# Cosine-weighted linear attention with a token-mixing layer: one load DMA of 576 KB in place of two of 288 KB

## The chip, the cores and the metric

The kernel runs on one core of a Trainium2 chip. The metric is the time of one execution on the device, in microseconds (us). A core has a matrix engine (TensorE, PE), a vector engine (VectorE, DVE), a scalar engine (ScalarE, ACT), a general engine (GpSimd, POOL) and an engine that here only issues transfers (SyncE, SP). Each runs its own instructions in order. The transfers themselves are carried by 16 DMA engines.

## The reference

Inputs are q, k and v of shape (batch 8, heads 8, positions 576, width 64) in float32, and three weights. The first stage is linear attention with cosine and sine weights on the positions, the second mixes tokens by products of two projections:

```python
theta = pi/2 * arange(576)/576
phi(x) = concat([relu(x)*cos(theta), relu(x)*sin(theta)], -1)
kv  = einsum('bhsf,bhsd->bhfd', phi(k), v);  z = sum(phi(k), axis=2)
x   = (phi(q) @ kv) / (phi(q) @ z + 1e-6)          # heads side by side: (8, 576, 512)
W   = (x @ w_q) @ (x @ w_k).T / sqrt(64)
out = relu(W @ x) @ w_out                          # (8, 576, 512) float32
```

## The kernel before

**Tiling.** The work is cut into 16 half batches, H = 0 to 15. A half batch is four heads of one batch, two pairs of heads. For each of q, k and v it has a raw tile of 128 partitions x 2 pairs x 576 float32 values (2304 B per partition and pair, 294912 B = 288 KB per pair). A pair of heads lies in DRAM as one contiguous block, 2304 B per partition; the two pairs of a half batch are two such blocks, one behind the other. Four raw tiles per tensor are used in turn (`NRAW` = 4), so the load of half batch H overwrites the tile of H - 4 and has to wait until that one was read.

**Stages of a half batch.** `L` loads (line 132). `RK`, `RQ` (relu to bf16, lines 187 and 189) and `CV` (cast, lines 193 and 195) read the raw tiles on ACT or POOL. `VS` (line 213, DVE) multiplies v by the table of cosines and sines; `QT` transposes q on PE, `QM` (line 253, DVE) weights it; `KV` (line 234, PE) forms the products of k and v, `KE` copies them out. `N` (line 269, PE) is the numerator with the denominator beside it, `EP` and `X` (lines 277 to 287) divide. Then, by batch: `XT` or `XR` transposes x and `XE` copies it, `WK`, `WQ`, `KX`, `MX` are matmuls of the second stage with copies `KW`, `QW`, `XK`, `XA`, `XB`, `ME` between them, `WO` (line 403, PE) is the product with the output weight, `OE` copies a 128 x 512 result into one of 12 output buffers, and `ST` (line 413) stores it (256 KB, 36 in all). `LW` loads the three weights (128, 128 and 1024 KB), `CW` casts them.

**Order.** The whole program is one list of words, `ORDER`, written out by hand or by a planner ahead of time and run through once. A word is a step, its index, the PSUM place (`:n`) and the engine (`@A`, `@V`, `@G`). Every engine takes its steps in the order of the list, and no step overtakes another on its engine. SP therefore has one order of loads and stores: a load whose tile is not yet free, or a store whose data isn't ready, holds all loads and stores behind it. Loads and stores together are 135 DMAs, all issued by SP.

**Halves.** Words with `a` or `b` (`LK0a`, `RK0b`) handle one pair of heads alone; they are used for half batch 0 only. Without it, `part` is `None`: a load then issues two DMAs, one per pair, and `RK`, `RQ`, `CV` and `VS` handle both pairs in one instruction. The list's first loads in SP's order are

```
LV1 LQ0b LQ1 LK1 LV0a LV0b LK0a LQ0a LK0b LV3 LQ3 LK3 LV2 LK2 LQ2 LV5 LW0 LW1 LK5 LQ4 LQ5 LV7 LV4
LQ7 LK4 LQ6 LW2 LV6 LK7 LV8 LK6 LV10 LQ8 LV9 LK10 LQ9 LK8 LK9 LQ11 LV11 LQ10 ST6 LK11 LV12 LK14 LK13
LV13 LQ12 LK12 LQ13 ST10 LV14 LV15 ST13 ST4 LQ14 ST3 LQ15 ST11 ST15 ST17 LK15 ST5 ...
```

and from there on only stores follow.

Of the kernel before, what the change touches and what calls it, by code (L numbers as in the profile page):

```python
# [63 lines left out]
def kernel(  # L64
# [10 lines left out]
    nc = tc.nc  # L75
# [18 lines left out]
    NRAW, NPREP, NV2, NQM, NX, NXT, NOUT = (4, 2, 2, 2, 2, 2, 12)  # L94
# [6 lines left out]
    def bufs(n, shape, dtype, name):  # L101
        return [pool.tile(shape, dtype, name=f"{name}{i}") for i in range(n)]

    raw = {nm: bufs(NRAW, [P, 2, HC], FP32, f"{nm}raw") for nm in "kqv"}
# [18 lines left out]
    def srcs(src):  # L123
        return [src[b].flatten().rearrange("(pr p e) -> p pr e", pr=NPAIR, p=P)
                for b in range(B)]

    src = {"k": srcs(k), "q": srcs(q), "v": srcs(v)}

    def load(nm, H, part):
        b, h = divmod(H, 2)  # L130
        for r in (0, 1) if part is None else (part,):
            nc.sync.dma_start(raw[nm][H % NRAW][:, r, :], src[nm][b][:, 2 * h + r, :])  # L132

# [300 lines left out]
    for word in ORDER.split():  # L434
        word, _, eng = word.partition("@")
        word, _, ps = word.partition(":")
        part = {"a": 0, "b": 1}.get(word[-1])
        word = word.rstrip("ab")
        kind = word[:2] if word[:2] in steps or word[0] in "LRCVT" else word[0]
        i, ps = int(word[len(kind):] or 0), int(ps or 0)  # L440
        if kind in ("LK", "LQ", "LV"):
            load(kind[1].lower(), i, part)
        elif kind in halves:
            halves[kind](i, ps, ENG.get(eng), slice(0, 2) if part is None else
                         slice(part, part + 1))
        else:
            steps[kind](i, ps, ENG.get(eng))
# [30 lines left out]
```

## Time and profile before

| | |
|---|---|
| time, median of 3 runs | 123.74 us (123.45 to 124.1) |
| the profiled execution | 122.49 us, of it a span of 120.7 us |
| granted TensorE clock | 0.991 of full speed |
| busy in the span | PE 94.8 us (79%), DVE 88.2 (73%), ACT 84.2 (70%), POOL 52.2 (43%) |
| moved | 39.40 MB, mean 326 GB/s |
| loads of q, k, v | 96 DMAs of 288 KB, median 5.9 to 6.0 us from issue to landing |
| stores | 36 DMAs of 256 KB, median 3.1 us |

The profile is one execution seen by the hardware's profiler. The span is the time from its first to its last instruction; the execution's own time is 1.8 us longer. In lines with instructions the first number is the start in us from the span's beginning, the second the duration, followed by the engine, the line of the kernel, the operation, and what it writes and reads; what stands in square brackets is idle time of the engine just before it and what ended it. A line of waits gives the total in us, how often, and the longest. SPq is SP's queue of DMA issues: a duration there is that of the issue, not of the transfer.

### The profile page before, as it was taken

The numbers are of one execution on the slowest core, as the hardware profiler recorded it, in microseconds if no ns is written. First come the engines' busy times: TensorE is split into PE (matmuls) and PEld (weight loads), VectorE is DVE, ScalarE is ACT, GpSimd is POOL, SyncE is SP. The second block draws the span as 40 slices with busy tenths as digits, with TensorE's granted clock in tenths as the row PEclk, the third lists the DMA queues.
The fourth block names the chain that finished last, engine by engine and source line by source line (L and its number), as shares of the span: only waits on it lengthen the run. The fifth ranks groups of instructions, "written<-read, shape, count | busy, mean of one in ns | idle before, by whom it ended". The sixth has DMA issues, their size and how long they took to land.

```text
span 120.7 us, 5301 instructions
## 1 busy us (share of the span) xinstructions
PE 94.8 (79%) x2286; PEld 63.1 (52%) x2286; DVE 88.2 (73%) x132; ACT 84.2 (70%) x155; POOL 52.2 (43%) x63
## 2 busy tenths in 40 slices
PE   0005919758778899969999999798999999999950
PEld 0004818637656656635667576454755864653410
DVE  0136998889989998997979987759969868766200
ACT  7246452967887989777967897586678668757450
POOL 2577136032739758146799304937365310010000
PEclk9999999999999999999999999999999999999996
DMA  3999999999999999999989999999997681875685
GB/s 111 318 384 405 395 391 391 361 405 396 392 390 408 398 337 344 355 360 379 383 282 326 364 285 391 343 331 283 391 299 263 238 329 55 320 288 198 237 331 196
DMA packets 20615, 39.40 MB, mean 326 GB/s; under 512 B 3184, under 2 KB 3184, under 8 KB 20592
## 3 DMA queue, kind: packets, MB, share of 16 engines
q1 hardware_dynamic: 20592, 39.07, 89.8%
q8 instruction: 18, 0.29, 1.0%
q14 instruction: 5, 0.04, 0.1%
HBM read 29.62 MB, written 9.44 MB: 324 GB/s over the span
## 4 chain that ended last, share of the span: by engine, by line
DMA 39%; PE 39%; DVE 6%; issue 4%; SPq 3%; ACT 3%; POOL 2%; DVEq 0%; ACTq 0%; POOLq 0%
DMA kraw<-in_k_dram 24%; PE ps L403 20%; DMA vraw<-in_v_dram 11%; DMA out_dram<-o 5%; PE ps L234 3%; PE ps L383 3%; PE ps L269 3%; SPq L132 3%; PE ps L360 3%; DVE v L213 2%; PE ps L313 2%; DVE x L287 2%; PE ps L245 2%; PE ps L333 2%; PE ps L346 2%
## 5 line engine op out<-in xcount | busy, mean ns | idle before, releaser
L403 PE MATMUL ps<-wow,mix 128*128 128x512 bf16 x144 | 34.7, 380 | 0.0
L287 DVE TENSOR_TENSOR x<-ps,rec 128x640 bf16<-128x640 f32 x32 | 26.4, 824 | 2.2
L195 POOL TENSOR_SCALAR vb<-vraw 128x1152 bf16<-128x1152 f32 (+1 forms) x16 | 17.9, 1122 | 20.9 <-DMA vraw<-in_v_dram 18.6
L213 DVE TENSOR_TENSOR v<-vb,vtab 128x2304 bf16<-128x2304 bf16 (+1 forms) x17 | 21.7, 1289 | 6.6 <-POOL vb L195 6.6
L253 DVE TENSOR_TENSOR qm<-ps,qtab 128x2304 bf16<-128x2304 bf16 x16 | 21.4, 1350 | 4.6 <-ACT qtab L166 2.9
L193 ACT COPY o<-ps 128x512 f32<-128x512 f32 x30 | 17.5, 587 | 6.6 <-PE ps L403 4.5
L269 PE MATMUL ps<-kvs,qm 64*128 64x65 bf16 x640 | 15.3, 199 | 6.0 <-ACT kvs L193 3.3
L403 PEld LDWEIGHTS <-mix 128*128 128x128 bf16 x144 | 12.4, 98 | 14.2 <-issue 0.9
L394 ACT ACTIVATE mix<-ps 128x576 bf16<-128x576 f32 x26 | 16.4, 657 | 3.2 <-PE ps L383 3.2
L189 POOL TENSOR_SCALAR rq<-qraw 128x1152 bf16<-128x1152 f32 x9 | 13.4, 1487 | 11.4 <-DMA qraw<-in_q_dram 10.8
L269 PEld LDWEIGHTS <-qm 64*128 64x128 bf16 x640 | 13.3, 100 | 9.4 <-issue 5.7
L189 POOL TENSOR_SCALAR rk<-kraw 128x1152 bf16<-128x1152 f32 (+1 forms) x12 | 13.8, 1150 | 9.4 <-DMA kraw<-in_k_dram 7.0
L193 ACT COPY xT<-ps 128x1280 bf16<-128x1280 bf16 (+1 forms) x13 | 15.4, 1186 | 3.3 <-PE ps L313 1.7
L234 PE MATMUL ps<-v,rk 64*64 64x130 bf16 x576 | 12.5, 236 | 3.0 <-DVE x L287 1.3
L245 PE MATMUL ps<-ident,rq 64*128 64x64 bf16 x288 | 7.6, 199 | 9.3 <-ACT rq L187 8.8
L187 ACT ACTIVATE rq<-qraw 128x1152 bf16<-128x1152 f32 (+1 forms) x8 | 8.4, 1046 | 6.6 <-DMA qraw<-in_q_dram 6.6
L234 PEld LDWEIGHTS <-rk 64*64 64x64 bf16 x576 | 10.1, 117 | 5.2 <-ACT rk L187 1.4
L245 PEld LDWEIGHTS <-rq 64*128 64x128 bf16 x288 | 6.1, 101 | 11.7 <-ACT rq L187 9.0
L383 PE MATMUL ps<-wq,kx 64*128 64x288 bf16 x64 | 8.3, 287 | 0.3 <-ACT xT L193 0.2
L195 POOL TENSOR_SCALAR kx<-kx 64x256 bf16<-64x256 bf16 x7 | 2.8, 399 | 12.6 <-ACT kx L193 12.2
L286 DVE RECIPROCAL rec<-rec 128x10 f32<-128x10 f32 x32 | 6.8, 211 | 1.8 <-ACT rec L277 1.4
L277 ACT ACTIVATE rec<-ps,eps 128x10 f32<-128x10 f32 x23 | 6.2, 273 | 1.7 <-PE ps L269 1.6
(46 smaller groups left out, 99.3 us busy)
## 6 DMA issues: line engine op xcount, KB each, us to landing
vraw<-in_v_dram SPq DMA_DIRECT2D x32, 288.0 KB, 6.0
qraw<-in_q_dram SPq DMA_DIRECT2D x32, 288.0 KB, 5.9
kraw<-in_k_dram SPq DMA_DIRECT2D x32, 288.0 KB, 5.9
out_dram<-o SPq DMA_DIRECT2D x36, 256.0 KB, 3.1
wof<-in_moe_w_out_dram SPq DMA_DIRECT2D x1, 1024.0 KB, 7.6
wqf<-in_moe_w_q_dram SPq DMA_DIRECT2D x1, 128.0 KB, 5.5
wkf<-in_moe_w_k_dram SPq DMA_DIRECT2D x1, 128.0 KB, 5.2
```

The costliest lines, as they stand in the source:

```text
L189: eng.tensor_scalar(dst, s, FMAX, 0.0, op0=ALU.min, op1=ALU.max)
L193: A.copy(dst, s)
L195: G.tensor_scalar(dst, s, 1.0, 1.0, op0=ALU.mult, op1=ALU.mult)
L213: V.tensor_mul(v2_b[H % NV2][:, part, :, :, 0:D], vb_b[H % NPREP][:, part].unsqueeze(3).to_broadcast([P, n, C, 2, D]), vtab.unsqueeze(1).t ...
L234: nc.tensor.matmul(kv_v[o, r, :], rk_b[H % NPREP][a, pr, c, :], v2_b[H % NV2][a, pr, c, :, 0:D + 1], start=(c == 0), stop=(c == C - 1))
L245: nc.tensor.transpose(qt_v[:, r, c * H2:(c + 1) * H2], rq_b[H % NPREP][a, c, :, :], ident[a, a])
L253: V.tensor_mul(qm_b[H % NQM][:, :, :, 0:C, :].rearrange("p s r c d -> p s r (c d)"), qt_view(place["QT", H]).unsqueeze(1).to_broadcast([P, ...
L269: nc.tensor.matmul(nv[:, pr, u, :], qm_b[H % NQM][a, s, r, 2 * u:2 * u + 2, :], kv_b[H % 2][a, r, s, 0:D + 1], start=(u == 0 and s == 0), ...
L287: V.tensor_tensor(x_b[b % NX][:, :, 4 * h:4 * h + 4, :].rearrange("p u (w r) d -> p r w u d", r=2)[:, r], nv[:, :, :, 0:D], rec.to_broadca ...
L383: nc.tensor.matmul(pair(ps)[:, t, :].bitcast(FP32)[:, 0:HS], kx_b[b % 2][a, (m // 2) ^ t, (m % 2) * P:(m % 2 + 1) * P], wq_b[b % 2][a, :], ...
L394: A.activation(dst, s, AF.Relu, scale=scale_moe)
L403: nc.tensor.matmul(o, mix_b[bp % 2][:, m, rt * P:(rt + 1) * P], wow[:, m, :], start=(m == 0), stop=(m == NDM - 1))
```

## The change

From half batch 2 on a load without a part is one DMA for both pairs of heads. Its destination is the whole raw tile, its source the two blocks of 2304 B per partition. Loads of half batches 0 and 1, the weights and the stores stay as they are, and so does the list. 42 loads are touched: 84 DMAs of 288 KB become 42 of 576 KB.

```diff
     def load(nm, H, part):
         b, h = divmod(H, 2)
+        if part is None and H > 1:
+            nc.sync.dma_start(raw[nm][H % NRAW], src[nm][b][:, 2 * h:2 * h + 2, :])
+            return
         for r in (0, 1) if part is None else (part,):
             nc.sync.dma_start(raw[nm][H % NRAW][:, r, :], src[nm][b][:, 2 * h + r, :])
```

## The prediction

> **What bounds the kernel now.** I read the page's slices first, to see which resource is full when; then the chain that ended last, to see which of them sets the end; then the waits of the DMA queue's issuer (SP), its issues in order of time, and the places where ACT, DVE and PE stand idle for a load.
>
> The page: busy tenths of PE and of the DMA engines in 40 slices of 3.02 us, what they moved, the shares of the chain, and the load issues.
>
> ```profile
> PE   0005919758778899969999999798999999999950
> DMA  3999999999999999999989999999997681875685
> GB/s 111 318 384 405 395 391 391 361 405 396 392 390 408 398 337 344 355 360 379 383 282 326 364 285 391 343 331 283 391 299 263 238 329 55 320 288 198 237 331 196
> DMA 39%; PE 39%; DVE 6%; issue 4%; SPq 3%; ACT 3%; POOL 2%; DVEq 0%; ACTq 0%; POOLq 0%
> kraw<-in_k_dram SPq DMA_DIRECT2D x32, 288.0 KB, 5.9
> ```
>
> Two regimes. Up to about 40 us the transfers run near 395 GB/s and PE is half idle; from about 50 us PE is full and transfers run at 280 to 390. The chain is loads until 32.8 us, compute until 61.6, loads again (64.4 to 76.4), one store (81.0 to 86.9), then PE.
>
> SP's waits (total us, times, longest), its issues in narrow windows, and steps of the chain (start, us):
>
> ```profile
> SPq L132 <- DMA qraw<-in_q_dram: 7.2, 19, 0.4
> SPq L132 <- DMA wof<-in_moe_w_out_dram: 2.2, 1, 2.2
> ...
> 10.75 0.33 SPq L132 DMA_DIRECT2D kraw<-in_k_dram  x1
> 16.01 0.33 SPq L132 DMA_DIRECT2D qraw<-in_q_dram  x1
> 37.19 0.33 SPq L132 DMA_DIRECT2D kraw<-in_k_dram  x1
> 39.71 0.33 SPq L132 DMA_DIRECT2D kraw<-in_k_dram  x1
> ...
> 26.28 6.51 DMA vraw<-in_v_dram
> 69.22 7.16 DMA kraw<-in_k_dram
> 81.00 5.93 DMA out_dram<-o
> ```
>
> SP waits for landings of loads that its next issue doesn't need as data. Counting the order out, the issue at 39.71 (second half of K6) is the eighth DMA after the 1 MB output weight, whose landing it waited for: a DMA is held until the one eight before it has landed. So eight are in flight, and 8 x 0.75 us is the 5.9 us to landing. The two K issues at 10.75 and the Q issue at 16.01 are seven places apart: (16.01 - 10.75) / 7 = 0.751 us for one 288 KB DMA, 393 GB/s. The issues at 37.19 and 39.71 follow two neighbouring landings, the second that of the 1 MB weight: 2.52 us, 416 GB/s.
>
> Where engines are idle for a load (DVE and ACT in order of time):
>
> ```profile
> 16.10 1.16 ACT L187 ACTIVATE rq<-qraw 128x1152 bf16<-128x1152 f32 x1 [2.41 <-DMA qraw<-in_q_dram]
> 21.13 1.16 ACT L187 ACTIVATE rk<-kraw 128x1152 bf16<-128x1152 f32 x1 [0.63 <-DMA kraw<-in_k_dram]
> 34.12 1.36 DVE L213 TENSOR_TENSOR v<-vb,vtab 128x2304 bf16<-128x2304 bf16 x1 [0.36 <-POOL vb L195]
> 76.49 1.16 ACT L187 ACTIVATE rk<-kraw 128x1152 bf16<-128x1152 f32 x1 [1.16 <-DMA kraw<-in_k_dram]
> 87.01 0.59 ACT L193 COPY o<-ps 128x512 f32<-128x512 f32 x1 [0.78 <-DMA out_dram<-o]
> ```
>
> These are RQ3, RK2, VS4 (through CV4 on POOL), RK12 and a copy into an output buffer whose store had not landed. They are short: loads are late by little.
>
> **The change part by part.** 84 DMAs of 288 KB become 42 of 576 KB. Bytes, order and readers stay. From the third half batch RK, RQ and CV each read both halves in one instruction, so no reader could use a first half before the second.
>
> *Transfer time.* Rate without overhead: (1048576 - 294912) B / (2.52 - 0.751) us = 426 GB/s; so a 288 KB DMA is 0.692 us of bytes and 0.059 us of its own. One 576 KB DMA then takes 1.443 us where two take 1.502: 0.059 us saved per load. Bounds: nothing saved, if the weight's rate comes from something else than its size; and below nothing, since eight DMAs before the landing at 76.38 (69.22 to 76.38) took 0.895 us each with the queue full: at that rate a load is 0.29 us slower. I take 0.059, because the weight is also one DMA of several separated rows per partition (four rows of 2048 B; here two of 2304 B), the nearest row. [...]
>
> *What that does to 34 us.* Two merged loads (V3, Q3) lie before RQ3: it starts 0.12 us earlier, and with it PE and DVE behind it. Five lie before K2 (0.30), but the KV matmuls behind RK2 then wait for DVE (0.77 us, PE's waits), so DVE keeps 0.12. Twelve lie before V4: it lands 12 x 0.059 = 0.71 us earlier. DVE arrives at VS4 0.12 us earlier and its 0.36 us of idle goes: 0.48 us, within the 0.71. Late next is DVE's own work. From 34 to 61 us the chain is DVE and PE; I carry the 0.48 through.
>
> *64 to 76 us.* SP is held at K14 until POOL's RK10 ends (64.0); that moves by the 0.48. Five merged loads (K14, K13, V13, Q12, K12) then lie before RK12: 5 x 0.059 = 0.30 us, against ACT's 1.16 us of idle before it and PE's 0.86 after it: 0.30 us more. If the queue never ran dry before K12 the bound is all 36 loads, 2.1 us.
>
> *The store at 81.0.* Three merged loads (V14, V15, Q14) are queued before it; it lands 0.18 us earlier against 0.78 us that ACT waits and PE waits behind ACT: 0.18 us.
>
> *Issues.* 42 issues of 0.33 to 0.43 us go from SP, 14 to 18 us. The three weight issues, with 512 rows each, took 0.38 us, so a 256-row issue should cost no more than 0.05 over a short one. I cost this at nothing: transfers queued for 3 us and more cover the issuer (least issue to landing of K: 4.0 us). Without that cover the two halves of a load start 0.43 us apart, and one DMA would gain that.
>
> *Depth.* Eight DMAs in flight are now up to 4.7 MB, not 2.4. In order, this gives nothing while the engines are full. It removes waits such as 0.6 us before the second half of K12 at 69.22, whose bytes stand behind seven others anyway: nothing. SP reaches waits for free buffers (V10 for CV6, 2.0 us; K10 for RK6, 1.9) and for output copies (ST6, ST10, ST13) sooner, but these end when compute ends them, and everything behind waits as now. Half batches 4 and 5 now need both halves of 0 and 1 read before their load; the last of those reads on ACT and POOL ended by 15 us, the loads go out after 16.
>
> *Tail.* From 88 us no load is issued; 28 stores follow PE. No change.
>
> Sum: 0.48 + 0.30 + 0.18 = 0.96 us. The profiled execution took 122.49 us (span 120.7 and 1.8 around it): 121.5. Against the median of 123.74, 1.25 above it: **122.8 us**.
>
> **The rivals.**
>
> *Hidden anyway.* The 0.059 us is the weight's own, or PE's queue absorbs the shift between 34 and 90 us, where PE idles only some 5 us and mostly for DVE and ACT. Then only VS4's stall or less goes: 0 to 0.4 us, 123.5. For it: DVE and PE each about nine tenths busy from 30 to 60 us. Against: the chain does start in loads.
>
> *More than that.* The DMA queue never ran dry, so K12 gains the whole 2.1 us: 121.6. Against: from 57 us SP is held by ST6 and RK10, and the rate falls to 282 GB/s.
>
> *Slower: a big load, or a deep queue, lands late.* If engines share their time among what is queued, or the fast ones of the 16 run ahead while a slow one lags, a load lands later the more is queued. Price: if the slow landing rate (0.29 us more per load) held for a third of the 12 loads before V4, 4 x 0.29 = 1.2 us: 124.9; for all of them, 3.5 us. It decides where a load takes over 1.55 us instead of 1.502 (12 x 0.05 = 0.6 us, half a percent). For it: between 72.3 and 75.0 us only two loads landed (CV13 and RQ12 on POOL start on them) though the slice there moved 391 GB/s, four loads' bytes; part of the engines ran ahead. Against it: at the start the third DMA had landed by 6.06 us (the issue there waited for it), with ten issued and about 1.3 MB, 4.4 DMAs, moved: the queue is served in order. [...]
>
> *Slower: halves that would have started sooner.* A whole load can't be confirmed before its last byte; should the last engine's lag grow with the size of one DMA, readers at RQ3, RK2, V4 and K12 start up to one half (0.75 us) later: +0.75, 124.5. Against: they wait for both halves today. [...]
>
> **How the numbers follow.** Forecast 0.46 (its own range 122.2 to 123.2), hidden 0.21, more 0.08, lands late 0.21, halves 0.04. What a measurement here can tell from no change is about 0.5%, 0.62 us, so "faster" is below 123.1. Faster: most of the forecast (0.42) and "more": 0.50. Same: the rest of the forecast, "hidden", and little of the others: 0.25. Slower: 0.25. The range reaches to "more", 121.6, and to the lower price of "lands late", 124.9; beyond lie its dearer part and extremes, under 0.2.
>
> **What would show it.** Right: 42 issues of 576 KB, landing about 8 to 12 us after issue; loads about 1.44 us apart before 35 us and 405 to 410 GB/s in those slices; VS4's 0.36 us idle gone and the instruction near 33.6 us; RK12's idle below 0.9 us; the tail from K15 on as long as now. Wrong: V4 landing after 32.8 us, slices below 390 GB/s before 35 us, stores to landing above 6 us, or PE idle for loads between 15 and 30 us where it waits for DVE today.

## The result and the profile after

The changed kernel took 130.26 us (median of 4 runs, 128.16 to 132.56) against 123.59 us before in the same comparison: 1.043 times the time before, 95% interval 1.030 to 1.057. It is slower, where 122.8 us was forecast, and lies beyond the range. Single runs scatter, those of the changed kernel by several us, so the ratios here set only the undisturbed runs of both kernels against each other, and the profiled run of the changed kernel (130.98 us, span 129.2 us) is not one of these.

The page of the changed kernel: busy tenths of PE, its granted clock, the DMA engines' busy share and what they moved, in 40 slices of 3.23 us, the chain by engines, and the queue that carries instructions.

```profile
PE   0026639649986896919999979898699999999960
PEclk9999999995999999975699999999999999999998
DMA  4999999999999999996007999798998195493794
GB/s 129 315 390 407 396 382 379 386 404 392 393 402 401 311 387 342 388 394 249 0 15 229 383 397 397 221 348 250 357 377 314 51 363 184 177 384 122 287 335 160
PE 66%; DMA 11%; issue 8%; DVE 5%; ACT 4%; SPq 2%; POOL 1%; ACTq 0%; POOLq 0%; DVEq 0%
q8 instruction: 18, 0.29, 0.9%
```

Three things are new: "issue" on the chain has doubled (4% to 8%: time in which an engine waited for nothing that the profile shows), PE's granted clock falls to 0.5 to 0.7 in the 18th to 20th slice (55 to 65 us, and once near 30 us), and in the 20th and 21st slice (61 to 68 us) the DMA engines stand almost still. The transfers of the first 40 us, which the forecast rested on, are as before. The rows of 10 to 40 us (columns: window, length, busy us of PE, PEld, DVE, ACT, POOL, granted clock, DMA share, GB/s), before and then after:

```profile
10.00:40.00 30.00, 21.70 (x680) 18.30 (x680) 27.02 (x42) 20.60 (x35) 13.70 (x13) 1.00 1.06 394
```

```profile
10.00:40.00 30.00, 22.15 (x640) 18.05 (x641) 26.06 (x40) 19.32 (x33) 12.18 (x13) 0.94 1.06 394
```

Where the time goes is seen in PE's instructions in order of time. All those that followed idle time without a visible cause, first before (2.0 us in sum), then after (7.1 us):

```profile
52.96 0.23 PE L313 MATMUL ps<-ident,x 64*128 64x64 bf16 x3 [1.01 <-issue]
68.26 0.34 PE L300 MATMUL ps<-ident,x 128*128 128x128 bf16 x3 [0.22 <-issue]
79.73 0.44 PE L245 MATMUL ps<-ident,rq 64*128 64x64 bf16 x18 [0.26 <-issue]
84.55 0.68 PE L346 MATMUL ps<-xT,wqw 128*64 128x288 bf16 x8 [0.53 <-issue]
```

```profile
44.81 0.40 PE L316 MATMUL ps<-ident,x 64*128 64x64 bf16 x15 [0.61 <-issue]
50.73 0.48 PE L272 MATMUL ps<-kvs,qm 64*128 64x65 bf16 x19 [1.05 <-issue]
57.75 0.29 PE L316 MATMUL ps<-ident,x 64*128 64x64 bf16 x3 [2.93 <-issue]
76.38 0.34 PE L303 MATMUL ps<-ident,x 128*128 128x128 bf16 x3 [0.80 <-issue]
83.03 0.30 PE L363 MATMUL ps<-x,wk 128*64 128x256 bf16 x2 [0.49 <-issue]
87.85 0.44 PE L248 MATMUL ps<-ident,rq 64*128 64x64 bf16 x18 [0.93 <-issue]
99.70 0.47 PE L248 MATMUL ps<-ident,rq 64*128 64x64 bf16 x20 [0.26 <-issue]
```

They break steps off in the middle: XR4 after 5 of its 20 matmuls, N14 after 1, XR7 after 17 (in both kernels). Counting matmuls along the list, XR4 begins after 730 of them, N14 after 862, XR7 after 974, so the breaks stand at matmul 735, 863 and 991; the later ones at 1375, 1502, 1630 and 1886. All are 94 or 95 above a multiple of 128, and a matmul is two instructions (weights and product, 2286 of each on the page): the stops stand 256 instructions, or a multiple of that, apart. PE's 2286 matmuls are 4572 instructions, 17.9 blocks of 256; the instruction queue moved 18 packets with 0.29 MB, 16 KB each, which the page counts to the 16 DMA engines' time (0.9%). From the two counts I take a packet to be one such block, and from the packets' times below that PE stands still until its next block has come, over the DMA engines that the loads fill (busy share 1.01 from 54 to 60 us).

The trace has the time of each of these packets. Around the longest stop, in us:

| | before | after |
|---|---|---|
| PE begins the block at matmul 863 | 47.86 | 50.73 |
| the next instruction packet starts | 50.50 | 55.24 |
| that packet ends | 51.42 | 56.14 |
| PE is through with its 128 matmuls | 51.95 | 54.82 |
| PE goes on at matmul 991 | 52.96 | 57.75 |

The packet takes 0.9 us in both kernels. It starts 4.51 us after PE began the block before, not 2.64, and these 1.87 us are nearly all of the 1.92 us by which the stop is longer. All eleven stops listed above end 1.3 to 1.6 us after the end of such a packet.

The same steps in both traces, start in us:

| step | before | after | later by |
|---|---|---|---|
| WQ0 | 29.01 | 29.64 | 0.63 |
| WQ1 | 35.71 | 36.98 | 1.27 |
| WQ2 | 45.38 | 47.25 | 1.87 |
| 12 matmuls of WO0, WO5, WO4 | 53.39 | 58.45 | 5.06 |
| MX9 behind them | 56.08 | 63.63 | 7.55 |
| end of the span | 120.7 | 129.2 | 8.5 |

From WQ2 to the WO matmuls 3.19 us are lost; the blocks at 863 and 991 cost 1.05 + 2.93 us where before they cost 1.01. The next 2.49 us are the WO matmuls themselves (before, then after):

```profile
53.39 2.76 PE L403 MATMUL ps<-wow,mix 128*128 128x512 bf16 x12
```

```profile
58.45 5.25 PE L406 MATMUL ps<-wow,mix 128*128 128x512 bf16 x12
```

They run at about half rate, after 2.93 us in which PE stood still; the granted clock of 60 to 66 us was 0.71. It had fallen to 0.50 at 56.7 us, 1.9 us after PE's last matmul, and stayed there until 63.5 us. What sets the moment is not shown, and a like stall does not always do it (below).

### The profile page after: what moved, and what is told of

Same layout as the page of the kernel before. It is cut to its first block, busy times and chain, and to the rows that moved or that the text cites. A ratio compares the mean times of both kernels' runs of the same rounds, so it can differ in the third digit from the quotient of the medians.

```text
span 129.2 us, 5239 instructions
## 1 busy us (share of the span) xinstructions
PE 98.2 (76%) x2286; PEld 64.1 (50%) x2286; DVE 89.9 (70%) x132; ACT 84.7 (66%) x155; POOL 51.9 (40%) x63
## 4 chain that ended last, share of the span: by engine, by line
PE 66%; DMA 11%; issue 8%; DVE 5%; ACT 4%; SPq 2%; POOL 1%; ACTq 0%; POOLq 0%; DVEq 0%
PE ps L406 28%; DMA kraw<-in_k_dram 11%; PE ps L272 7%; PE ps L237 7%; PE ps L363 4%; PE ps L349 4%; PE ps L386 4%; PE ps L336 3%; PE ps L316 3%; PE ps L248 3%; DVE x L290 3%; PE ps L303 2%; SPq L135 2%; ACT xT L196 1%; DVE qm L256 1%
## 5 line engine op out<-in xcount | busy, mean ns | idle before, releaser
L406 PE MATMUL ps<-wow,mix 128*128 128x512 bf16 x144 | 37.2, 401 | 0.0
L216 DVE TENSOR_TENSOR v<-vb,vtab 128x2304 bf16<-128x2304 bf16 (+1 forms) x17 | 23.0, 1363 | 5.6 <-POOL vb L198 5.6
L198 POOL TENSOR_SCALAR vb<-vraw 128x1152 bf16<-128x1152 f32 (+1 forms) x16 | 17.9, 1121 | 20.2 <-DMA vraw<-in_v_dram 15.4
L406 PEld LDWEIGHTS <-mix 128*128 128x128 bf16 x144 | 12.9, 101 | 15.8 <-issue 3.7
L192 POOL TENSOR_SCALAR rk<-kraw 128x1152 bf16<-128x1152 f32 (+1 forms) x12 | 14.9, 1240 | 13.6 <-DMA kraw<-in_k_dram 12.1
L272 PE MATMUL ps<-kvs,qm 64*128 64x65 bf16 x640 | 14.8, 197 | 6.4 <-ACT kvs L196 3.1
L272 PEld LDWEIGHTS <-qm 64*128 64x128 bf16 x640 | 12.8, 98 | 9.7 <-issue 6.2
L192 POOL TENSOR_SCALAR rq<-qraw 128x1152 bf16<-128x1152 f32 x9 | 11.4, 1266 | 13.8 <-DMA qraw<-in_q_dram 6.8
L198 POOL TENSOR_SCALAR kx<-kx 64x256 bf16<-64x256 bf16 x7 | 3.3, 470 | 14.4 <-ACT kx L196 14.1
L316 PE MATMUL ps<-ident,x 64*128 64x64 bf16 x220 | 5.6, 195 | 3.6 <-issue 3.5
```

The costliest lines, as they stand in the source:

```text
L192: eng.tensor_scalar(dst, s, FMAX, 0.0, op0=ALU.min, op1=ALU.max)
L198: G.tensor_scalar(dst, s, 1.0, 1.0, op0=ALU.mult, op1=ALU.mult)
L216: V.tensor_mul(v2_b[H % NV2][:, part, :, :, 0:D], vb_b[H % NPREP][:, part].unsqueeze(3).to_broadcast([P, n, C, 2, D]), vtab.unsqueeze(1).t ...
L272: nc.tensor.matmul(nv[:, pr, u, :], qm_b[H % NQM][a, s, r, 2 * u:2 * u + 2, :], kv_b[H % 2][a, r, s, 0:D + 1], start=(u == 0 and s == 0), ...
L406: nc.tensor.matmul(o, mix_b[bp % 2][:, m, rt * P:(rt + 1) * P], wow[:, m, :], start=(m == 0), stop=(m == NDM - 1))
```

## The experiments

Each batch of runs shared the runs of the kernel before on its chip; those had medians of 124.26 us (m_sp1, m_sp2, b_sp1, b_sp2), 125.75 (b_sp4, m_early, m_late, m_shift) and 125.74 (the others). "Stalls" are PE's stalls without visible cause of 0.2 us and more, summed over the one profiled run of a kernel.

**Fewer bytes in flight, same merged loads.** Behind each merged load SP issues an extra DMA of 256 B into a tile that nobody reads. As a DMA waits for the landing of the eighth before it (in the kernel before, every load issued from 6 to 40 us goes out 0.02 to 0.24 us after that landing), four of the eight in flight are then loads. In the second kernel the extra DMA follows every second load.

```diff
             nc.sync.dma_start(raw[nm][H % NRAW], src[nm][b][:, 2 * h:2 * h + 2, :])
+            spacer(1)        # m_sp2: spacer(2), every second time
             return
+    def spacer(every): ...
+            nc.sync.dma_start(spc[:, spn[1], :], moe_w_q[0:16, 0:4])
```

> The merged loads stay; behind each of them SP issues one extra DMA of 256 B that nobody reads. Of the eight DMAs in flight four are then loads, 2.4 MB as before the change, not 4.7. Theory A (depth: PE's instructions come over the same DMA engines, 256 at a time, and wait behind what is queued): the stalls of PE at every 256th instruction fall from 7.1 us to 3 us or less, no clock drop, 123 to 125 us. Theory B (one load of 576 KB, or its two rows per partition, lands late by itself): nothing changes, 128 us or more.

> The merged loads stay; an extra DMA of 256 B that nobody reads behind every second one, so that some 5.3 loads (3.1 MB) are in flight. Theory A: between the two, page stalls of PE of 2 to 5 us, 124 to 127 us. Theory B: 128 us or more.

m_sp1: 124.73 us (123.35 to 126.2), ratio 1.003, interval 0.994 to 1.012. The only stall left is at block 991:

```profile
54.74 0.23 PE L327 MATMUL ps<-ident,x 64*128 64x64 bf16 x3 [1.05 <-issue]
```

m_sp2: 127.35 us (124.73 to 127.81), stalls 6.6 us, above the 2 to 5 us expected. One of its four runs took 124.73 us and the others 127.1 to 127.8, so there is no ratio, and what its depth costs in time is not shown. Merged loads with the old depth cost nothing that can be measured (at most 1.2%), so size and pattern of the loads don't make the 4%; of what the change does, the depth is left.

**Fewer bytes in flight than before.** The same extra DMA in the kernel before, behind every second or every 288 KB load from half batch 2 on; and behind every fourth, for half batches 8 to 15 alone.

```diff
         for r in (0, 1) if part is None else (part,):
             nc.sync.dma_start(raw[nm][H % NRAW][:, r, :], src[nm][b][:, 2 * h + r, :])
+            if H > 1:
+                spacer(2)    # b_sp1: spacer(1); b_sp4: H > 7, spacer(4)
```

> The loads of before (288 KB); from half batch 2 on an extra DMA of 256 B that nobody reads behind every second one, so that some 5.3 of them (1.6 MB, not 2.4) are in flight. Theory A: PE's page stalls fall below the 2.0 us of before, 122 to 124 us. Theory B: no change of the stalls, 123.5 to 125 us for the extra issues.

> The loads of before; an extra DMA of 256 B that nobody reads behind each one from half batch 2 on, so that 4 of them (1.2 MB) are in flight. Theory A: page stalls of PE under 1 us, but the transfers may fall below 390 GB/s early: 122 to 126 us. Theory B: 124 to 127 us, stalls as before.

> The loads of before; for half batches 8 to 15 alone an extra DMA of 256 B that nobody reads behind every fourth DMA, so that some 6.4 loads (1.9 MB, not 2.4) are in flight there. Theory A: page stalls between the 2.0 us of before and the 0.9 us seen with 1.6 MB, and no loss of transfers before 40 us: 122.3 to 124.3 us. If the extra DMAs themselves cost transfers, 125 us or more.

| kernel | MB in flight, by the count of eight | stalls, us | median, us |
|---|---|---|---|
| b_sp1 | 1.2 | 0 | 146.92 |
| b_sp2 | 1.6 | 0.7 | 133.40 |
| b_sp4 (late loads) | 1.9 | 1.3 | 127.16 (before there 125.75) |
| before | 2.4 | 2.0 | 123.59 |
| m_sp1 | 2.4 | 1.0 | 124.73 |
| m_sp2 | 3.1 | 6.6 | 127.35 |
| changed | 4.7 | 7.1 | 130.26 |

The count of eight gives the most that can be in flight. From issue to landing, the changed kernel had 4.0 MB in flight on average from 10 to 40 us and 2.8 MB from 42 to 58 us, the kernel before 2.5 and 2.1 MB. The stalls went as theory A has them, in two groups: 2.0 us and less up to 2.4 MB, 6.6 us and more above. Within a group the order is not shown, since two profiled runs of one kernel (m_early and m_early2, below) had 0.5 and 2.9 us. In b_sp2 and b_sp1 PE also runs fewer matmuls (593 and 522 from 10 to 40 us, before 680), so that a late block shows less. The times did not follow: b_sp2 is 1.076 (1.069 to 1.084) and b_sp1 1.185 (1.178 to 1.193) times before, since the transfers then starve. The windows of 10 to 40 us, b_sp2 and then b_sp1:

```profile
10.00:40.00 30.00, 19.51 (x593) 16.57 (x595) 24.73 (x37) 18.90 (x31) 9.63 (x10) 0.89 0.98 328
```

```profile
10.00:40.00 30.00, 18.89 (x522) 16.31 (x523) 21.63 (x34) 16.10 (x26) 8.84 (x9) 0.89 0.90 282
```

328 and 282 GB/s instead of 394. Part of that may be the extra DMAs themselves: m_sp1 issues as many as b_sp2 (42) and, at the old depth, moved 359 GB/s in this window, though it lost no time. Of the depths tried, none was better than the old one. b_sp4 (124.34 to 128.31, before on that chip 121.46 to 128.94) lies above the 122.3 to 124.3 us expected and shows no gain, though it moved 392 GB/s from 10 to 40 us.

**One part of the change alone.** Merging only half batches 2 to 7, or only 8 to 15.

```diff
-        if part is None and H > 1:
+        if part is None and 1 < H < 8:      # m_late: H > 7
```

> Loads merged only for half batches 2 to 7 (the loads of the first 40 us); 8 to 15 stay two DMAs. Theory A: PE needs a block of 256 instructions only every 7 us or more in that time, so a late block hardly shows; later the queue is as deep as before the change: page stalls near 2 us, 123 to 125.5 us, of it up to 0.7 us because K3 lands at 18.3 and not 17.6 us. Theory B (big loads land late and the early ones set the chain): 127 us or more.

> Loads merged only for half batches 8 to 15; 2 to 7 stay two DMAs. Theory A: the page stalls of PE after 44 us come back in the main: 4 to 7 us in sum, the largest at the block that begins at matmul 991; 126 to 130 us. Theory B: 123 to 125 us.

> Merged loads for half batches 2 to 7 only, once more with more rounds, against before. Theory A: the same as before within 1%: the queue is as deep as before where PE needs its blocks fast, and the 0.06 us per early load is hidden behind DVE. 122.5 to 125 us.

m_late: 128.82 us (126.52 to 130.27), stalls 8.0 us, more than the 4 to 7 us expected. m_early: 124.46 us (122.81 to 125.06), stalls 0.5 us, while before had 125.75 (121.46 to 128.94) on that chip, too wide for a ratio. On the same chip every run of m_late took longer than every run of m_early. With more runs (m_early2) the median was 125.10, the ratio 1.012 (1.007 to 1.018), a little above the 1% expected; stalls 2.9 us. So most of the loss sits in the late loads, and the early ones bring no gain, rather 1% of loss, whose place I did not find. In m_late the largest stall is at block 863, not at 991 as expected:

```profile
52.53 0.73 PE L272 MATMUL ps<-kvs,qm 64*128 64x65 bf16 x19 [2.69 <-issue]
53.19 1.19 PE L237 MATMUL ps<-v,rk 64*64 64x130 bf16 x36
```

The KV step behind it takes 1.19 us, not 0.72: a low clock again (0.86 on average from 48 to 54 and from 54 to 60 us). Its trace also has a low clock in parts of 18 to 32 us (0.67 on average from 20 to 30 us), where its loads are those of before; the low clock near 30 us in the changed kernel's trace (0.50 from 29.4 to 32.8 us) therefore needs no merged loads.

**Is it the blocks?** 32 idle matmuls at the start of PE's program, where it waits for data, in the changed kernel.

```diff
     def TI(i, ps, eng):
+        for n in range(32):
+            nc.tensor.matmul(PS[0:D, 7, :].bitcast(FP32)[:, 0:D], vtab[:, 0, 0, :],
+                             vtab[:, 0, 1, :], start=True, stop=True)
         make_identity(nc, ident)
```

> All loads merged as in the change; 32 extra matmuls on PE (64 instructions) at the very start, where PE waits for its first data, so that every later instruction stands 64 places further back. In the changed kernel the stalls of PE without a visible cause stand at matmuls 735, 863, 991, 1375, 1503, 1631, 1887, all 95 or 96 above a multiple of 128, that is 256 instructions apart. Theory A (blocks of 256 instructions arrive late): the same stalls now come 32 matmuls of the kernel's own earlier, at 703, 831, 959 and so on (63 above a multiple of 128, the extra ones not counted), in sum 4 to 9 us. If they belong to the steps where they stand, they stay at 735, 863, 991. 126 to 133 us.

127.82 us (one run), stalls 7.1 us. Those up to 75 us:

```profile
43.88 0.45 PE L306 MATMUL ps<-ident,x 128*128 128x128 bf16 x5 [1.51 <-issue]
50.62 0.33 PE L275 MATMUL ps<-kvs,qm 64*128 64x65 bf16 x9 [1.42 <-issue]
56.82 0.36 PE L275 MATMUL ps<-kvs,qm 64*128 64x65 bf16 x11 [2.53 <-issue]
73.20 0.23 PE L319 MATMUL ps<-ident,x 64*128 64x64 bf16 x3 [0.84 <-issue]
```

The first now breaks XT5 after 5 of 10 (698 + 5 = 703), the next N15 after 11 (831), then N13 after 9 (959) and XR9 after 17 (1343): each 32 matmuls earlier in the kernel's own count, as theory A has it. XR4, N14 and XR7 run through. The stall belongs to the place in the instruction stream, not to the step. The 2.53 us at 959 were not followed by a low clock here: the four WO matmuls at 57.11 us took 1.04 us, as those at 46.26 us did.

The packets agree over all traces. The longest time from PE's start of a block to the start of the next instruction packet, the last packet left out, was 4.2 to 5.2 us in the five traces whose late loads are all merged with no extra DMA (the changed kernel, m_late, m_shift, and m_again and m_st6 below), and 2.0 to 3.9 us in the other nine.

**Is it the hole in the transfers?** The two empty slices tempt one to another reading (theory C): SP waits for ST6, whose output copy is late, and holds eight loads (K11 to Q13; the expectation says nine, and idle DMA engines from 57.8 us, where they moved data until about 61). In m_st6 the store stands behind them. Its buffer is by then refilled by OE10, so one output tile of 128 rows holds those of another; all steps and their sizes stay. e_st6 is the same with only half batches 2 to 7 merged.

```diff
-... XK3@A ST6 MX8:4 XB3@V N19:0 LK11 ... LQ13 XK4@A ...
+... XK3@A MX8:4 XB3@V N19:0 LK11 ... LQ13 ST6 XK4@A ...
```

> The changed kernel once more, as the measure for the next one on the same chip. Page stalls of PE 5 to 9 us in sum, all 256 instructions apart, 127 to 132 us.

> The changed kernel with the first store, ST6, moved in the list from before LK11 to behind LQ13. SP then doesn't hold the nine loads from K11 to Q13 back for the output copy OE6, which in the changed kernel left the DMA engines idle from 57.8 to 66.9 us. Theory A (PE's late instruction blocks): the hole closes, but PE has work through it, so the time stays that of the changed kernel within 1.5 us, or rises, as the deep queue now lasts through the next blocks. Theory C (the time is lost in the hole, as the loads behind it come late): 3 us or more below the changed kernel.

> Merged loads for half batches 2 to 7 and ST6 moved behind LQ13. Theory A: loads from K11 on come earlier, which takes ACT's 1.2 us wait for K12 away, but the queue stays full longer while PE is dense: 122 to 125 us, page stalls 1 to 3 us. Theory C: 1 us or more faster than before.

m_again, the changed kernel once more: 128.12 us, ratio 1.040 (1.026 to 1.055), stalls 5.3 us. m_st6: 127.72 us, ratio 1.042 (1.036 to 1.047), stalls 4.7 us. The windows of 60 to 66 us, m_again and then m_st6:

```profile
60.00:66.00 6.00, 5.95 (x148) 3.64 (x147) 5.45 (x6) 5.18 (x10) 4.43 (x4) 1.00 0.10 35
```

```profile
60.00:66.00 6.00, 5.95 (x156) 3.87 (x157) 4.52 (x5) 4.87 (x10) 5.00 (x4) 1.00 0.78 293
```

The DMA share went from 0.10 to 0.78 and the time did not move: PE is full in that window either way. The hole is an effect of PE's lateness (OE6 waits for PE), not its cause. It is a part answer, as six of the eight loads were then held by another wait (K14 for POOL's RK10, up to 10.7 us). e_st6: 125.60 us, ratio 1.023 (1.014 to 1.032), stalls 2.6 us: no gain either, and theory C's 1 us faster did not come.

## Why the prediction was wrong

*Depth* is the step that failed. It costed eight DMAs of 576 KB in flight at "nothing", as served in order, and so never late. For loads and stores that held; but the instruction blocks of PE come as packets over DMA engines too (18 of 16 KB, 0.9% of the time of the 16), and the prediction's list of who waits left them out. The sign was on the page shown: "issue" 4% of the chain, and the trace had the 1.01 us at 52.96 in the middle of a step. Measured, the depth costs 5 us of stalls in the profiled pair (2.0 to 7.1), plus 2.5 us of half clock behind the longest, and it accounts for the loss: with the depth put back (m_sp1) the ratio is 1.003. The split between stalls and clock differs from run to run: m_st6, at 127.62 us, has 4.7 us of stalls and no half clock behind the longest. A block's packet takes no longer in the deep queue, it starts later: before the longest stop 4.51 us after PE began the block before, not 2.64. When a block is asked for the trace doesn't show, so what holds its packet back stays open.

*Transfer time*, 0.059 us saved per load: not there. Both kernels move 394 GB/s from 10 to 40 us. Four merged loads landed 1.49 us apart (28.49 to 34.46 us), not 1.44, while the 1 MB weight again took 2.50 us, so its rate does not carry over to loads of 576 KB; of the bounds, "nothing saved" came nearest. CV4, which starts on V4's landing, was to come 0.71 us earlier; before and then after:

```profile
32.93 1.15 POOL L195 TENSOR_SCALAR vb<-vraw 128x1152 bf16<-128x1152 f32 x1 [0.33 <-DMA vraw<-in_v_dram]
```

```profile
33.03 1.15 POOL L198 TENSOR_SCALAR vb<-vraw 128x1152 bf16<-128x1152 f32 x1 [0.28 <-DMA vraw<-in_v_dram]
```

V4 landed at 32.95 us, past the 32.8 that the prediction named as a sign of being wrong, but only 0.17 us later than before. With that the three gains (0.48, 0.30 and 0.18 us) have nothing under them. RQ3 did start 0.31 us earlier (15.79), RK3 0.81 us later (18.46); in m_late, whose early loads are those of before, RK3 also stood at 18.12, 2.63 us after RQ3 (before 1.55), and in m_early, with merged early loads, at 17.57, so that lateness is not the merging's.

*Issues*: 0.37 us for a merged load where the queue has room, as said. Where it has not, SP stood in one issue for several us (below). That it was covered by transfers holds for SP's loads.

*Tail*: from the issue of the last load (K15) to the end of the span 36.3 us (from 92.9), before 35.1 (from 85.6), so nearly unchanged: what was lost was lost earlier.

*Rivals*: "lands late" had the sign and the cause's first half, a deep queue, with the wrong victim and a price of 1.2 us where 4.3%, 5.3 us, came. Up to V4 loads landed late by some tenths at most, K3 by 0.8. Its deciding point, loads over 1.55 us, was not reached and the time rose all the same. "Halves" fell with m_sp1, which merges them too. "Hidden anyway" is what m_sp1 shows of the merging by itself.

In the profiled runs the stalls at the blocks' boundaries were 0 to 2.9 us in sum up to 2.4 MB in flight behind the late loads, 6.6 at 3.1 MB and 4.7 to 8.0 at 4.7 MB.

## What to carry to other kernels

How deep loads are queued can be a price for what else comes over the DMA engines, here the instructions of a busy engine (2.0 us of stalls at 2.4 MB in flight, 7.1 at 4.7): count PE's instructions along the list, and look whether its idle time without visible cause stands a fixed number of them apart, here 256. A change to the size of DMAs also changes the bytes in flight where their number is what is limited (here eight); separate the two with a cheap extra DMA before judging either. A hole in the transfers next to a full PE can be the effect and not the cause, as it was here; moving what waits in it tells.

## What the runs showed that I had not expected

With large DMAs in the queue SP itself is held in the issue (SP's issues in order of time in the changed kernel):

```profile
12.69 1.23 SPq L420 DMA_DIRECT2D wqf<-in_moe_w_q_dram  x1
14.19 2.91 SPq L422 DMA_DIRECT2D wkf<-in_moe_w_k_dram  x1
17.20 3.33 SPq L132 DMA_DIRECT2D kraw<-in_k_dram  x1
```

K5 took 3.33 us to issue; the longest issue before was 1.75. The limit is then no longer the eighth DMA back (for K5 that had landed 1.52 us before the issue began), and a load lands 9.1 to 9.6 us (median) after its issue, not the 12 that eight times 1.5 us would give.

The length of a stall alone doesn't decide on the low clock: stalls of 2.93 us (changed kernel, 0.50 from 56.7 to 63.5 us), 2.69 (m_late, 0.86 on average from 54 to 60 us) and 2.42 (m_again, 0.82 from 54 to 60 us) were followed by it, those of 2.53 (m_shift) and 2.38 (m_st6, 1.00 from 54 to 66 us) were not. What decides it, and how much of the scatter of the changed kernel's runs comes from it, was not tried.
